# Seven products of a feature transform in another order, with their operands loaded in fewer transfers

## The chip, the cores and the metric

The kernel runs on one core of one Trainium2 chip. The metric is device time in microseconds of one launch. A core has TensorE (PE in the profile, with its weight loads as PEld), VectorE (DVE), ScalarE (ACT), GpSimd (POOL) and SyncE (SP). SP issues nearly all transfers between the chip's memory and the on-chip tiles.

## The reference

Two mixers of the same tokens are blended by a gate. S is 2048 tokens, D 640 features, H 32 heads of 20.

```python
g = sigmoid((x * gate_w).sum(-1, keepdims=True))
qkv = x @ wqkv                                  # 32 heads of 20
o = softmax(q @ k.T * 20 ** -0.5) @ v           # per head
a = o @ wo
A, B = x @ hid_re.T, x @ hid_im.T               # transform of the features
b = seq_re @ A - seq_im @ B                     # transform of the tokens
out = g * a + (1 - g) * b
```

## The kernel before

**Stages.** A prologue (to about 228 us) makes q, k and v, stores them, and makes the right operands of the feature transform. Then comes one long loop of 256 cycles, which carries the attention of all 16 pairs of heads; the transforms are filled into it. A cycle takes the order of its work from the string `ORDER`: `e` is a score matmul with its exponential (L1069, L1075), `m` a score matmul for the maxima of a later unit (L191, L193), `F` a place for one or more groups of transform matmuls, and `B` the burst of sixteen matmuls with v (L714) that closes the cycle. A pair of heads takes 16 cycles of four steps each. The score matmuls of `m` run 43 steps ahead of those of `e` (`LEAD`), so they come to the next pair of heads at the start of the sixth of the sixteen cycles.

**The feature transform** fills the first 56 cycles. It is computed by seven products of half-size blocks in place of eight, as in the known seven-product scheme for matrices. `FEATURE` has a row for each product: the terms of its left operand (sign, half of the tokens, half of the features of x), the terms of its right operand (of the transform's matrices), a factor, and its targets (sign, half of the tokens, real or imaginary part). A product takes eight cycles: the first four with the first half of the columns, the last four with the second. In each cycle `hid_pair` runs 30 matmuls of L498, for one of four blocks of rows. Each product therefore uses two right operands, called sets here (0 to 13).

**Left operands** (tile x from the tiles part). `load_left` is called at a product's first cycle for the next product. It loads the terms of x (in_xh) in three pieces of 1024, 1024 and 512 columns, and works them off in five slabs of 512 columns in the product's first six cycles: with two terms GpSimd adds them (L445), then it splits the sum in a rounded part and a rest (L130, L131).

**Right operands** (tile wb). The prologue made them and stored them in w_scr. `load_right` loads a set, 1600 KB, while the set before it is in use; there are two tiles, so a load can start when the matmuls with the set before that are done, and it has the four cycles of one set to land.

**Targets.** ScalarE and VectorE take the result out of the accumulators. Two of the four targets (half and part both 0, or both 1) are kept on the chip as tiles x and summed by GpSimd (L511). The other two go to memory (a_scr). Where such a target has a value already, this *old value* is loaded into one of three slots (part<-a_scr, 320 KB) at the pair's cycle, added to, and stored again about ten steps later; the load three pairs later, which takes the slot again, waits for that store.

**The k, q and v of the next pair of heads** are loaded at the start of every sixteenth cycle, so at the start of the first, third, fifth and seventh product: six loads each of k and q (kst and qst, 160 KB each), and one of v. They are in the queue from the moment that the scores have done with the tile.

**What sets the order of transfers.** All of them go through one queue, SP's, in the order in which the program wrote them: `at_step` puts an issue at a step of the loop. SP issues each as soon as what it waits for is there, and everything behind it waits as well. Lines 1004 (before) and 1006 (after) are only where `begin` carries out what was put at a step.

Of the kernel before, what the change touches and what calls it, by code (L numbers as in the profile page):

```python
# [13 lines left out]
ALU = mybir.AluOpType  # L14
# [4 lines left out]
P = 128  # L19
# [4 lines left out]
ND = D // P  # L24
# [38 lines left out]
FEATURE = (  # L63
# [7 lines left out]
)  # L71
SETS = 2 * len(FEATURE)
# [11 lines left out]
def f32(ap):  # L84
    return ap.bitcast(F32)
# [3 lines left out]
def mix_kernel(ctx: ExitStack, tc: tile.TileContext, xa, xh, wqk, wb, wr, cdft, wo, out):  # L89
    nc = tc.nc  # L90
    pe, act, dve, pool, sp = nc.tensor, nc.scalar, nc.vector, nc.gpsimd, nc.sync
# [59 lines left out]
    def raw_tile():  # L151
        return work.tile([P, 1024], F32, name="raw", bufs=3)
# [24 lines left out]
    def at_step(i, fn):  # L177
        later.setdefault(i, []).append(fn)
# [243 lines left out]
    def load_right(k):  # L422
        w = wide.tile([P, 2, ND, BW], R, name="wb", bufs=2).rearrange("p z d c -> p (z d c)")[:, : 2 * RW]
        w = w.rearrange("p (z c) -> p z c", z=2)
        rights[k] = w.rearrange("p z (d c) -> p z d c", d=ND)
        return [functools.partial(sp.dma_start, f32(w)[64 * h : 64 * h + 64, z], w_scr[k, z]) for z in range(2) for h in range(2)]

    stages = []

    def load_left(n, stage):  # L430
        terms = FEATURE[n][0]
        hi, lo = [block(z, 2 + n % 2) for z in range(2)]

        def load(q):
            c = slice(1024 * q, min(1024 * q + 1024, ND * 512))
            raws = stage(q)
            for raw, (_, th, dh) in zip(raws, terms):
                sp.dma_start(raw[:, : c.stop - c.start], xh[th, dh, :, c])
            return raws

        def slab(j, raws):
            c = slice(512 * j, 512 * j + 512)
            a, b = [raw[:, j % 2 * 512 : j % 2 * 512 + 512] for raw in raws]
            if len(terms) > 1:
                pool.tensor_tensor(a, a, b, op=ALU.add if terms[1][0] > 0 else ALU.subtract)  # L445
            split(hi[:, c], lo[:, c], a, pool, pool)

        lefts[n] = [l.rearrange("p (d c) -> p d c", d=ND) for l in (hi, lo)]
        raws = {}

        def step_(j):
            def fn():
                if j < 2:
                    raws[j] = load(j)
                if j:
                    slab(j - 1, raws[(j - 1) // 2])
                if j == 2:
                    raws[2] = load(2)
            return fn

        return [step_(j) for j in range(ND + 1)]

    def own_stage(q):
        return [f32(stages[q % 2])[:, z] for z in range(2)]

    def raw_stage(q):
        return [raw_tile()] * 2

    def acc(ri, hf, k):
        if (ri, hf) not in accs:  # L470
# [5 lines left out]
    def hid_pair(u):  # L476
        n, hf, k = u // 8, u // 4 % 2, u % 4
        _, _, factor, targets = FEATURE[n]
        ps = [new_y(z)[:, :HE] for z in range(2)]
        fresh = [(th, ri, hf, k) not in seen for _, th, ri in targets]  # L480
        seen.update((th, ri, hf, k) for _, th, ri in targets)
        rows = [a_scr[ri, hf, th, k] for _, th, ri in targets]
        olds = []
        for (_, th, ri), new, row in zip(targets, fresh, rows):
            old = None
            if th == ri:
                old = acc(ri, hf, k)
            elif not new:
                old = slots.pop(0)
                slots.append(old)  # L490
                at_step(now[0] + 4, functools.partial(sp.dma_start, old, row))
            olds.append(old)
        done_ = 0
        for d in range(ND):
            for a, b in ((0, 0), (0, 1), (1, 0)):
                for z in range(2):
                    r = slice(64 * z, 64 * z + 64)
                    pe.matmul(ps[z], lefts[n][a][r, d, k * P : k * P + P], rights[2 * n + hf][r, b, d],  # L498
                              start=done_ == 0, stop=done_ == 3 * ND - 1)
                done_ += 1  # L500
                if done_ < 3 * ND:
                    yield
        direct = [i for i, ((_, th, ri), new) in enumerate(zip(targets, fresh)) if new and th == ri]
        m = olds[direct[0]] if direct else raw_tile()[:, : 2 * HE].rearrange("p (s c) -> p s c", s=2)

        def read():
            act.activation(m[:, 0], ps[0], AF.Copy, scale=factor)
            dve.tensor_scalar(m[:, 1], ps[1], factor, 1.0, op0=ALU.mult, op1=ALU.mult)  # L508

        def add(sign, old):  # L510
            pool.tensor_tensor(old, old, m, op=ALU.add if sign > 0 else ALU.subtract)  # L511

        extras.append((now[0], read))
        last = n == len(FEATURE) - 1
        for (sign, th, ri), new, row, old in zip(targets, fresh, rows, olds):
            if not new:
                extras.append((now[0] + 3, functools.partial(add, sign, old)))
            if th != ri or ri == 0 and n == len(FEATURE) - 2 or ri == 1 and last:
                at_step(now[0] + (4 if new else 11), functools.partial(sp.dma_start, row, m if new else old))
        yield  # L520

# [64 lines left out]
    for m, (n, t) in enumerate(tiles):  # L586
        qk_pairs(order[n], t, m)
        if m == 8:
            load_v(0)
        if m == 4:  # L590
            sets = load_weights(1)
            queue_sets()
        if n < 5 and t == 1:
            fin()
            if n + 3 < len(order):
                fin = load_wqk(order[n + 3], pool)
        if m == 19:
# [29 lines left out]
    at = {}  # L627
# [610 lines left out]
```

## Time and profile before

| | us |
|---|---|
| runs: median of 3 (lowest to highest) | 1882.21 (1882.14 to 1882.55) |
| the profiled execution, device time | 1880.69 |
| its span, first to last instruction | 1878.8 |
| TensorE busy | 1845.9 (98%) |
| VectorE busy | 1459.4 (78%) |
| GpSimd busy | 1300.1 (69%) |
| ScalarE busy | 1237.4 (66%) |
| TensorE waiting for wb at L498 | 23.4, in 4 waits |

A row of the timeline has the start in us from the span's beginning, the duration in us, the engine, the line, the operation, what it writes and reads (tile<-tiles), and how many instructions were merged in it (x16). In brackets stands how long the engine was idle before, and what ended that. SPq is SP's queue: a row there is the issue of a transfer, and how long the issue took, not the transfer itself. In the list of transfers, KB is 1024 bytes.

A row of a list of waits has who waited for whom, the total in us, the number of waits and the longest.

A row of a table by windows has the window, its length, the busy time of TensorE, its weight loads, VectorE, ScalarE and GpSimd (each with its number of instructions), the TensorE clock that was granted, the busy share of the transfer engines and the GB/s that they moved.

### The profile page before, as it was taken

What the parts mean: (1) busy time and instruction counts of PE and PEld (TensorE: products, weight loads), DVE (VectorE), ACT (ScalarE), POOL (GpSimd) and SP (SyncE); (2) the same over time, 40 slices, a digit from 0 to 9 for tenths busy, and PEclk for the clock granted to TensorE, in tenths of its full rate; (3) what the DMA queues carried; (4) which work ended last, traced back from release to release, by engine and by line L of the source; (5) the groups of instructions that cost most, each with busy time, mean ns of one, the idle gap of its engine ahead of it and who ended that gap; (6) DMA issues with size and microseconds to landing.
All of it is one profiled execution on the core that took longest, in us unless ns stands there. A gap on an engine that the chain in (4) does not pass through costs nothing. (4 is left out here: it accounts for less than half of the span.)

```text
span 1878.8 us, 45939 instructions
## 1 busy us (share of the span) xinstructions
PE 1845.9 (98%) x17917; PEld 1344.8 (72%) x17917; DVE 1459.4 (78%) x2428; ACT 1237.4 (66%) x2378; POOL 1300.1 (69%) x1098
## 2 busy tenths in 40 slices
PE   9999999898899999999999999999999999999998
PEld 8988977675576777767677776677767677776666
DVE  4157589787687888888888888888888888889953
ACT  4233477676576676767677676667767667677785
POOL 1379535573775999466799889968779987734344
PEclk9999999999899999999999999999999999999999
DMA  7887874877776674546557586647486756542224
GB/s 233 202 271 283 270 214 114 193 228 179 201 202 181 207 232 150 159 132 181 183 161 248 156 246 184 196 126 205 138 231 212 209 176 169 167 107 70 63 56 152
DMA packets 195133, 342.26 MB, mean 182 GB/s; under 512 B 54639, under 2 KB 108015, under 8 KB 194659
## 3 DMA queue, kind: packets, MB, share of 16 engines
q1 hardware_dynamic: 193955, 337.35, 61.5%
q0 software_dynamic: 960, 1.97, 0.6%
q8 instruction: 141, 2.31, 0.5%
q14 instruction: 77, 0.63, 0.1%
HBM read 257.79 MB, written 81.28 MB: 180 GB/s over the span
## 5 line engine op out<-in xcount | busy, mean ns | idle before, releaser
L193 DVE TENSOR_REDUCE mx<-ps 128x1 f32<-128x512 f32 x2048 | 1299.7, 686 | 232.4 <-PE ps L191 211.0
L1075 ACT ACTIVATE p<-ps 128x512 f32<-128x512 f32 x2048 | 1088.4, 598 | 454.4 <-PE ps L191 223.5
L191 PE MATMUL ps<-kst,qst 60*128 60x512 f32 x2048 | 778.4, 414 | 2.0 <-DVE mx L193 1.4
L1069 PE MATMUL ps<-qst,kst 62*128 62x512 f32 x2048 | 697.4, 415 | 0.0
L795 PE MATMUL yp<-x,part 64*128 64x320 f32 x5376 | 643.0, 306 | 0.0
L795 PEld LDWEIGHTS yp<-x,part 64*128 64x128 f32 x5376 | 580.7, 186 | 7.4
L1069 PEld LDWEIGHTS ps<-qst,kst 62*128 62x128 f32 x2048 | 334.5, 185 | 222.6 <-DVE mx L193 129.8
L714 PE MATMUL av<-p,v 128*21 128x512 f32 x4096 | 492.5, 596 | 0.0
L191 PEld LDWEIGHTS ps<-kst,qst 60*128 60x128 f32 x2048 | 368.5, 185 | 14.2 <-DVE mx L193 1.6
L131 POOL TENSOR_TENSOR part<-raw,part 128x1024 fp32r<-128x1024 f32 (+3 forms) x134 | 297.1, 2217 | 10.2
L714 PEld LDWEIGHTS av<-p,v 128*21 128x21 f32 x4096 | 95.3, 100 | 207.5 <-issue 206.9
L498 PE MATMUL yp<-wb,x 64*128 64x320 f32 x1680 | 214.7, 314 | 23.4 <-DMA wb<-w_scr 23.4
L130 POOL CAST part<-raw 128x1024 fp32r<-128x1024 f32 (+2 forms) x127 | 125.2, 986 | 131.9 <-PE yp L795 100.7
L656 POOL TENSOR_TENSOR raw<-raw,raw 128x1024 f32<-128x1024 f32 x78 | 187.2, 2400 | 33.4 <-DMA raw<-in_cdft 18.1
L498 PEld LDWEIGHTS yp<-wb,x 64*128 64x128 f32 x1680 | 186.4, 191 | 27.9 <-DMA wb<-w_scr 24.7
L131 POOL TENSOR_TENSOR x<-araw,x 128x320 fp32r<-128x320 f32 x96 | 84.0, 875 | 7.7
L866 PE MATMUL yp<-x,part 64*128 64x320 f32 x720 | 87.3, 309 | 0.0
L883 POOL TENSOR_TENSOR x<-x,m 128x320 f32<-128x320 f32 x30 | 26.2, 874 | 81.0 <-DVE m L878 62.5
L511 POOL TENSOR_TENSOR x<-x,raw 128x640 f32<-128x640 f32 x40 | 62.5, 1563 | 22.8 <-DVE raw L508 16.0
L866 PEld LDWEIGHTS yp<-x,part 64*128 64x128 f32 x720 | 75.7, 185 | 2.6
L689 POOL TENSOR_TENSOR araw<-araw 128x320 f32<-128x320 f32 x80 | 70.1, 876 | 3.2 <-DMA araw<-a_scr 3.2
L511 POOL TENSOR_TENSOR part<-part,raw 128x640 f32<-128x640 f32 x16 | 25.0, 1563 | 53.5 <-DMA part<-a_scr 34.7
(107 smaller groups left out, 1402.5 us busy)
## 6 DMA issues: line engine op xcount, KB each, us to landing
raw<-in_cdft SPq DMA_DIRECT2D x189, 512.0 KB
araw<-a_scr SPq DMA_DIRECT2D x176, 160.0 KB
wb<-w_scr SPq DMA_DIRECT2D x56, 400.0 KB
qk_scr<-p SPq DMA_DIRECT2D x40, 512.0 KB
kst<-qk_scr SPq DMA_DIRECT2D x90, 160.0 KB
qst<-qk_scr SPq DMA_DIRECT2D x90, 160.0 KB
part<-in_xh SPq DMA_DIRECT2D x22, 512.0 KB
yt<-y_scr SPq DMA_DIRECT2D x64, 160.0 KB
```

The costliest lines, as they stand in the source:

```text
L130: e1.tensor_copy(dst1, src)
L131: e2.tensor_tensor(dst2, src, f32(dst1), op=ALU.subtract)
L191: pe.matmul(ps, q[b : b + KROWS, qt * P : (qt + 1) * P], k[b : b + KROWS, kc * 512 : (kc + 1) * 512], start=True, stop=True)
L193: return lambda: dve.tensor_reduce(mx[n][:, h, qt, kc : kc + 1], ps, axis=AX.X, op=ALU.max)
L498: pe.matmul(ps[z], lefts[n][a][r, d, k * P : k * P + P], rights[2 * n + hf][r, b, d], start=done_ == 0, stop=done_ == 3 * ND - 1)
L511: pool.tensor_tensor(old, old, m, op=ALU.add if sign > 0 else ALU.subtract)
L656: pool.tensor_tensor(raws[0], raws[0], raws[1], op=ALU.add if PRODUCTS[n][0][1][0] > 0 else ALU.subtract)
L714: pe.matmul(av[32 * j : 32 * j + DH + 1, :], v[:, kt, h * (DH + 1) : (h + 1) * (DH + 1)], pp[qc][:, h, :], start=kt == 0, stop=kt == NS - 1)
L795: pe.matmul(yp[h][:, :HE], c[r, cz, cs], a[r, az], start=s == 0 and z == 0, stop=s == NS - 1 and z == 2)
L866: pe.matmul(yp[h][:, :HE], o[r, oz, d], wos[d, hf][r, wz], start=d == 0 and z == 0, stop=d == ND - 2 and z == 2)
L1069: pe.matmul(pt, k[b : b + KROWS + 2, kt * P : (kt + 1) * P], q[b : b + KROWS + 2, qc * 512 : (qc + 1) * 512], start=True, stop=True)
L1075: act.activation(pts[n, kt, qc][:, h], pt, AF.Exp, scale=float(DH) ** -0.5)
```

## The change

The products stand in another order: the fifth becomes the third, the third the fourth, the sixth the fifth, and the fourth the sixth. With it, the old values are loaded in the fourth and sixth product; before, in the third and fifth. A right operand is loaded in two transfers of 800 KB, one for each half of the partitions, instead of four of 400 KB, and the second stands four steps behind the first. Both terms of a left operand come in one transfer for each piece. A target that stays on the chip is stored when its last product is done, which a small table now tells.

```diff
 FEATURE = (
     (((1, 1, 1),), ((1, 1, 0), (-1, 0, 0)), 1.0, ((1, 0, 0), (1, 1, 0))),
     (((1, 0, 0), (1, 1, 1)), ((1, 0, 0), (-1, 1, 1)), 1.0, ((1, 0, 0), (1, 1, 1))),
+    (((1, 0, 0), (1, 0, 1)), ((1, 1, 1),), -1.0, ((-1, 0, 0), (1, 0, 1))),
     (((1, 1, 0), (1, 1, 1)), ((1, 0, 0),), 1.0, ((1, 1, 0), (-1, 1, 1))),
+    (((1, 0, 1), (-1, 1, 1)), ((1, 1, 0), (-1, 1, 1)), 1.0, ((1, 0, 0),)),
     (((1, 0, 0),), ((1, 1, 1), (-1, 0, 1)), 1.0, ((1, 0, 1), (1, 1, 1))),
-    (((1, 0, 0), (1, 0, 1)), ((1, 1, 1),), -1.0, ((-1, 0, 0), (1, 0, 1))),
-    (((1, 0, 1), (-1, 1, 1)), ((1, 1, 0), (-1, 1, 1)), 1.0, ((1, 0, 0),)),
...
# load_right
-        return [functools.partial(sp.dma_start, f32(w)[64 * h : 64 * h + 64, z], w_scr[k, z]) for z in range(2) for h in range(2)]
+        return [functools.partial(sp.dma_start, f32(w)[64 * h : 64 * h + 64], w_scr[k].rearrange("z r c -> r z c")) for h in range(2)]
...
# load_left
-            raws = stage(q)
-            for raw, (_, th, dh) in zip(raws, terms):
-                sp.dma_start(raw[:, : c.stop - c.start], xh[th, dh, :, c])
+            raws = stage(q)[:, : len(terms), : c.stop - c.start]
+            at = sorted(2 * th + dh for _, th, dh in terms)
+            sp.dma_start(raws, xh[at[0] : at[-1] + 1 : max(at[-1] - at[0], 1), :, c].rearrange("t p c -> p t c"))
...
# hid_pair
-        last = n == len(FEATURE) - 1
+        ends_ = {(th, ri): i for i, f in enumerate(FEATURE) for _, th, ri in f[3]}
...
-            if th != ri or ri == 0 and n == len(FEATURE) - 2 or ri == 1 and last:
+            if th != ri or ends_[th, ri] == n:
...
# prologue
-        if 20 <= m < 28:
+        if 20 <= m < 28 and m % 2 == 0:
             chunks.pop(0)()
...
# end
-                        at_step(i + 1 + 3 * q, fn)
+                        at_step(i + 1 + 4 * q, fn)
```

What this does to SP's queue is seen at three places. The first is the start of the third product. Ahead of these rows stand four or five loads of k, one piece of x, the first part of wb, and v. Before (wb is the right operand, in_xh is x, qk_scr holds k and q, a_scr the targets):

```order
L1004 DMA wb<-w_scr 64x1600
L438 DMA part<-in_xh 128x1024
L1004 DMA kst_91<-qk_scr 20x4x512
L1004 DMA qst_93<-qk_scr 20x4x512 x2
L1004 DMA wb<-w_scr 64x1600
L1004 DMA part<-a_scr 128x640
L1004 DMA qst_93<-qk_scr 20x4x512
L731 DMA lc<-l_scr 128x16
L438 DMA part<-in_xh 128x512
L1004 DMA qst_93<-qk_scr 20x4x512 x2
L1004 DMA wb<-w_scr 64x1600
L1004 DMA qst_93<-qk_scr 20x4x512
```

The same stretch now:

```order
L438 DMA part<-in_xh 128x2x1024
L1006 DMA kst_91<-qk_scr 20x4x512
L1006 DMA wb<-w_scr 64x2x1600
L1006 DMA a_scr<-raw 128x640
L1006 DMA qst_93<-qk_scr 20x4x512 x3
L733 DMA lc<-l_scr 128x16
L438 DMA part<-in_xh 128x2x512
L1006 DMA qst_93<-qk_scr 20x4x512
L1006 DMA a_scr<-raw 128x640
L1006 DMA qst_93<-qk_scr 20x4x512 x2
```

The last part of wb stood behind five loads of q and two old values; now it stands ahead of all loads of q. The pieces of x have two terms here instead of one, stores of a new target have come in, and the loads of old values are gone.

The second place is the start of the fifth product. Before:

```order
L438 DMA part<-in_xh 128x1024 x2
L1004 DMA a_scr<-raw 128x640
L1004 DMA kst_92<-qk_scr 20x4x512
L1004 DMA wb<-w_scr 64x1600
L1004 DMA kst_92<-qk_scr 20x4x512 x2
L1004 DMA part<-a_scr 128x640
L558 DMA v<-v_scr 128x672
L1004 DMA kst_92<-qk_scr 20x4x512
L728 DMA l_scr<-o 4x512
L1004 DMA wb<-w_scr 64x1600
L438 DMA part<-in_xh 128x1024 x2
```

Now:

```order
L438 DMA part<-in_xh 128x1024
L1006 DMA kst_92<-qk_scr 20x4x512
L1006 DMA wb<-w_scr 64x2x1600
L1006 DMA kst_92<-qk_scr 20x4x512 x2
L1006 DMA a_scr<-part 128x640
L560 DMA v<-v_scr 128x672
L1006 DMA kst_92<-qk_scr 20x4x512
L730 DMA l_scr<-o 4x512
L438 DMA part<-in_xh 128x1024
L1006 DMA kst_92<-qk_scr 20x4x512
L1006 DMA wb<-w_scr 64x2x1600
```

x has one term here now, and in the place of the loads of old values stand stores of those that the fourth product added to.

The third place is the start of the seventh product, where pieces of a for the token transform (part<-a_scr 128x4x320, 640 KB) are loaded as well. Before:

```order
L1004 DMA wb<-w_scr 64x1600
L697 DMA part<-a_scr 128x4x320
L1004 DMA kst_91<-qk_scr 20x4x512
L1004 DMA qst_93<-qk_scr 20x4x512 x2
L1004 DMA wb<-w_scr 64x1600
L1004 DMA a_scr<-x_3090 128x640
L1004 DMA qst_93<-qk_scr 20x4x512
L731 DMA lc<-l_scr 128x16
L1004 DMA qst_93<-qk_scr 20x4x512 x2
L1004 DMA wb<-w_scr 64x1600
L1004 DMA qst_93<-qk_scr 20x4x512
```

Now, from a little further ahead:

```order
L1006 DMA part<-a_scr 128x640
L1006 DMA a_scr<-part 128x640
L1006 DMA kst_91<-qk_scr 20x4x512 x2
L1006 DMA wb<-w_scr 64x2x1600
L1006 DMA kst_91<-qk_scr 20x4x512 x2
L1006 DMA a_scr<-part 128x640
L560 DMA v<-v_scr 128x672
L1006 DMA kst_91<-qk_scr 20x4x512
L730 DMA l_scr<-o 4x512
L699 DMA part<-a_scr 128x4x320
L1006 DMA kst_91<-qk_scr 20x4x512
L1006 DMA wb<-w_scr 64x2x1600
```

The last load of an old value of the sixth product has come in ahead of the loads of k, and the second half of wb stands ahead of all loads of q, where the last quarter stood behind five of them.

More of the change, by code (lines that the diff above doesn't have):

```diff
@@ L442, in slab @@
             c = slice(512 * j, 512 * j + 512)
-            a, b = [raw[:, j % 2 * 512 : j % 2 * 512 + 512] for raw in raws]
+            parts = [raws[:, z, j % 2 * 512 : j % 2 * 512 + 512] for z in range(len(terms))]
+            a = parts[0]
             if len(terms) > 1:
-                pool.tensor_tensor(a, a, b, op=ALU.add if terms[1][0] > 0 else ALU.subtract)
+                one, two = parts if terms[0][1:] < terms[1][1:] else parts[::-1]
+                pool.tensor_tensor(a, one, two, op=ALU.add if terms[1][0] > 0 else ALU.subtract)
             split(hi[:, c], lo[:, c], a, pool, pool)
@@ L463, in own_stage @@
     def own_stage(q):
-        return [f32(stages[q % 2])[:, z] for z in range(2)]
+        return f32(stages[q % 2])
     def raw_stage(q):
-        return [raw_tile()] * 2
+        return raw_tile().rearrange("p (z c) -> p z c", z=1)
     def acc(ri, hf, k):
@@ L1214 @@
     wqk = w[:, : 2 * D].reshape(ND, P, 2 * ND, P).transpose(2, 1, 0, 3)
-    xh = np.asarray(A_x)[0].reshape(2, 2, 512, 2, ND, 64).transpose(0, 3, 1, 5, 4, 2).reshape(2, 2, P, ND * 512)
+    xh = np.asarray(A_x)[0].reshape(2, 2, 512, 2, ND, 64).transpose(0, 3, 1, 5, 4, 2).reshape(4, P, ND * 512)
     wr = np.stack([np.asarray(m) for m in (B_dft_hid_re, B_dft_hid_im)])
```

## The prediction

> **What bounds the kernel now.** I read the span first, then whom TensorE waits for, then its timeline around each of those waits.
>
> ```profile
> span 1878.8 us, 45939 instructions
> PE yp L498 <- DMA wb<-w_scr: 23.4, 4, 8.8
> ```
>
> TensorE is the bound, and over the span it waits for one thing worth speaking of: a right operand of the feature products (wb, read by the matmuls of L498), four times, 23.4 us. A cycle ends with sixteen matmuls of L714, so the distance between two such rows is the length of a cycle.
>
> ```profile
> 346.69 1.92 PE L714 MATMUL av<-p,v 128*21 128x512 f32 x16
> 352.94 1.92 PE L714 MATMUL av<-p,v 128*21 128x512 f32 x16
> 361.52 1.43 PE L498 MATMUL yp<-wb,x 64*128 64x320 f32 x7 [5.72 <-DMA wb<-w_scr]
> 366.69 1.92 PE L714 MATMUL av<-p,v 128*21 128x512 f32 x16
> ...
> 460.69 1.92 PE L714 MATMUL av<-p,v 128*21 128x512 f32 x16
> 468.23 0.63 PE L498 MATMUL yp<-wb,x 64*128 64x320 f32 x1 [4.83 <-DMA wb<-w_scr]
> 477.67 1.43 PE L498 MATMUL yp<-wb,x 64*128 64x320 f32 x7 [8.80 <-DMA wb<-w_scr]
> 482.80 0.63 PE L714 MATMUL av<-p,v 128*21 128x512 f32 x4
> ...
> 576.91 1.92 PE L714 MATMUL av<-p,v 128*21 128x512 f32 x16
> 583.80 1.43 PE L498 MATMUL yp<-wb,x 64*128 64x320 f32 x7 [4.01 <-DMA wb<-w_scr]
> 590.24 1.05 PE L714 MATMUL av<-p,v 128*21 128x512 f32 x8
> ...
> 353.00:366.70 13.70, 7.98 (x65) 5.85 (x64) 5.65 (x11) 4.76 (x9) 8.65 (x8) 0.75 0.65 153
> ```
>
> A plain cycle is 6.25 us (346.69 to 352.94). Three cycles, in the third, fifth and seventh product, take 13.75, 22.11 and 13.33 us: 7.50, 15.86 and 7.08 too long, **30.4 us together**. The waits in them are 5.72, 13.63 and 4.01; the other 1.78, 2.23 and 3.07 (mean 2.4) is slow work after each wait: the last row (PEclk is the third number from its end) has a granted clock of 0.75 in the long cycle.
>
> Why the operand is late stands in the timeline of the queue that issues it.
>
> ```profile
> 326.50 0.29 SPq L1004 DMA_DIRECT2D kst<-qk_scr  x1
> ...
> 350.36 0.45 SPq L1004 DMA_DIRECT2D wb<-w_scr  x1
> 352.53 0.28 SPq L1004 DMA_DIRECT2D qst<-qk_scr  x1
> 353.67 0.34 SPq L1004 DMA_DIRECT2D part<-a_scr  x1
> 354.48 3.01 SPq L752 DMA_DIRECT2D o_scr<-o  x4
> 358.52 0.35 SPq L1004 DMA_DIRECT2D a_scr<-part  x1
> 364.12 0.34 SPq L1004 DMA_DIRECT2D part<-a_scr  x1
> SPq L752 <- DMA part<-in_xh: 4.5, 5, 1.5
> ```
>
> The last quarter of wb is issued at 350.36 and lets TensorE go at 361.52, 11.2 us later. Seven issues follow it and then none until it has landed; and a store of o_scr waits for x to land, which it has no use for (last row). So SP keeps eight transfers under way and issues the next when the one eight places before lands. The queue is full, and what counts is how many bytes stand ahead.
>
> ```profile
> kst<-qk_scr SPq DMA_DIRECT2D x90, 160.0 KB
> wb<-w_scr SPq DMA_DIRECT2D x56, 400.0 KB
> part<-in_xh SPq DMA_DIRECT2D x22, 512.0 KB
> part<-a_scr SPq DMA_DIRECT2D x16, 320.0 KB
> v<-v_scr SPq DMA_DIRECT2D x16, 336.0 KB
> part<-a_scr SPq DMA_DIRECT2D x4, 640.0 KB
> ```
>
> From the first k load (326.50) to 361.52 these landed: 11 k and q loads 1760 KB, x 1280, wb 1600, two old values 640, v 336, two of 8: 5632 KB in 35.0 us, **161 KB/us**. The fifth product has two terms of x and a store more: 7232 KB from 434.35 to 477.67, **167 KB/us**. The seventh, from 548.11 to 583.80, has four stores, three pieces of a of 640 KB, 11 k and q loads, wb and v: 6912 KB, **194 KB/us**.
>
> ```profile
> 434.35 0.29 SPq L1004 DMA_DIRECT2D kst<-qk_scr  x1
> ...
> 548.11 0.37 SPq L1004 DMA_DIRECT2D a_scr<-x  x1
> ```
>
> **The change, part by part.** *Fewer, larger transfers.* 28 wb issues and 15 of x go; the bytes stay. SP's own issuing (0.3 to 0.5 us a row) is hidden, since in the bad stretches SP waits for landings. What it brings is position: both halves of wb now stand ahead of all q loads, and count for two places of the eight instead of four.
>
> *Old values out of the third and fifth product.* They met the k, q and v loads there; the fourth and sixth have none. I price each stretch by its bytes.
>
> Third product, to the second half of wb: 6 k loads 960, x in two parts of 1024, wb 1600, v 336, l 8: 4952 KB. It must land by 355.80 (361.52 less 5.72), 29.3 us after 326.50, which takes 169 KB/us. At 161 it is 1.5 us late, at 167 it is 0.4 late, at the 183 found below 2.2 early. I take: in time.
>
> But the third product now prepares a left operand of two terms, 1280 KB more of x, and **the q loads are late next**. The scores of L191, which run ahead, read the new k and q from the start of the sixth cycle of an odd product. The first product shows it:
>
> ```profile
> 230.89 0.40 SPq L1004 DMA_DIRECT2D kst<-qk_scr  x1
> ...
> 249.39 1.95 SPq L1004 DMA_DIRECT2D qst<-qk_scr  x2
> ...
> 260.64 0.50 PE L191 MATMUL ps<-kst,qst 60*128 60x512 f32 x1
> ...
> 390.00:415.00 25.00, 25.00 (x250) 17.22 (x248) 21.79 (x37) 18.20 (x37) 22.51 (x19) 1.00 0.93 293
> ```
>
> There 12 k and q loads, x 2560, v and two stores, 5456 KB, were in by 260.64, since TensorE did not wait: at most 29.75 us, at least **183 KB/us**. The third product gets exactly this and wb on top: 7072 KB with l and lc. Its sixth cycle would start at 352.94 + 6.25 + 1.85 = 361.04, so it has 34.5 us, and needs 205 KB/us. Low end: wb's 1600 KB at the 286 KB/us (293 GB/s, last row) of a stretch without k and q add 5.6 us to 29.75: 0.8 us late. High end: all at 161: 9.4 late. I take 183, since the mix is the first product's: 38.6 us, **4.1 late**, and with 2.4 of slow work **6.5 us**. Before, the last q load was issued behind the last wb (352.53 against 350.36, above), so it landed after 361.52 and was late too, covered by the wait for wb.
>
> [...]
>
> Fifth product: one term of x (1280), no old values after its k loads but two stores: 5792 KB in the same 34.5 us. At 161: 1.5 late; at 167: 0.2; at 183: 2.9 early. I take 0.
>
> Seventh: no change but one old value left from the sixth (320 KB), and the last q load counted: 7392 KB from 548.11. At its own 194: 586.2, and needed at 576.91 + 6.25 + 1.85 = 585.0: **1.2 late**, at 183 3.5 late, at 205 early. A wait this short I take without slow work after it.
>
> [...]
>
> *Fourth and sixth product* now carry eight old loads and eight stores each beside wb and x, without k and q; the stretch of 293 GB/s has stores, wb and x, so I price them at nothing. If that cover is gone, the nearest price is the shortest of the three losses, 7.08 a product. *Left operand on GpSimd:* the same instructions in all, two terms in products 2, 3, 4, 5 and 7. *The loads in the prologue* come two places earlier; TensorE has no wait for them.
>
> Sum against the profiled execution's 1880.69: less 30.4, plus 6.5, 0 and 1.2: **1858.0**. The median of the runs, 1882.21, lies 1.5 above that execution, which is inside the range.
>
> **Rivals.** *Everything hidden.* The first product landed before 260.64, how much is not seen; with 4 us of slack there nothing waits. For it: the fewer places held by wb. Against: wb beside k and q went at 161 and 167. 1880.69 - 30.4 = 1850.3.
>
> *The old rate stays.* wb and k, q share the engines as before, at 161 KB/us: third 9.4 + 2.4, fifth 1.5, seventh 3.5 + 2.4 = 19.2 left, 1869.5. For it: two stretches measured it. Against: both held old values, whose loads wait for stores.
>
> *Slower, by GpSimd.* Its queue is in order, and an addition waits for the old value:
>
> ```profile
> 452.15 1.57 POOL L511 TENSOR_TENSOR part<-part,raw 128x640 f32<-128x640 f32 x1 [5.91 <-DMA part<-a_scr]
> 453.68 1.28 POOL L445 TENSOR_TENSOR part<-part 128x512 f32<-128x512 f32 x1
> 455.02 0.62 POOL L130 CAST x<-part 128x512 fp32r<-128x512 f32 x1
> 455.72 1.29 POOL L131 TENSOR_TENSOR x<-part,x 128x512 fp32r<-128x512 f32 x1
> ...
> 469.12 1.53 POOL L511 TENSOR_TENSOR part<-part,raw 128x640 f32<-128x640 f32 x1 [10.59 <-DMA part<-a_scr]
> ```
>
> The fourth and sixth product have 16 additions (1.57) and five slabs (3.19): 41.1 of 50 us. Waits of 5.91 and 10.59 through all eight pairs, 33 us in pairs of two, would end them 24 late; the slabs are queued in the first six of eight cycles, so two (12.5) absorb half, and the next left operand stops TensorE for 11.5 + 2.4 in each: 27.8, with the 19.2 above 47.0, against 30.4 gained: 1897.3. It decides from about 18 us late on. Against: both waits fell under k and q loads.
>
> *It does nothing:* the wait moves whole to the next late load, 1880; nothing in the bytes says so.
>
> **How the numbers follow.** Forecast, 1853 to 1863: 0.48. All hidden: 0.25. Old rate: 0.20. GpSimd: 0.04. Nothing: 0.03. The range reaches from all hidden to just under the old rate, **1850 to 1868**. A difference of 0.2% (3.8 us) is what the measurement can tell; faster 0.94, same 0.02, slower 0.04.
>
> **What would show it.** Right: no waits of L498 for wb; one wait of L191, or of the matmuls beside it, for qst in the sixth cycle of the third product, some 4 us, and a cycle of about 12.7 us there; the fifth product plain. All hidden: every cycle 6.25. Old rate: that cycle near 18 us, and wb late too. GpSimd: TensorE waits for x at L498. Wrong is the argument by bytes if the fourth or sixth product waits, where no k and q are loaded.

## The result, and the profile after

| | before | after |
|---|---|---|
| median of 10 runs each, us | 1882.18 (1874.82 to 1885.65) | 1872.46 (1868.36 to 1879.49) |
| profiled execution, its device time, us | 1880.69 | 1871.42 |
| its span, us | 1878.8 | 1869.6 |

The ratio of after to before is 0.9955, with an interval of 0.9941 to 0.997: about 9.7 us less, where 22.7 were forecast (from the 1880.69 of the profiled execution to 1858.0). The time lies above the predicted range of 1850 to 1868.

The head of the list of TensorE's waits after the change:

```profile
core 0 of [0], span 1869.6 us
engine line waited for: us in total, times, longest us
PE ps L191 <- DVE mx L193: 10.8, 4, 5.9
PE yp L500 <- ACT raw L509: 3.3, 2, 2.7
PE yp L500 <- DMA wb<-w_scr: 1.6, 1, 1.6
```

In this execution the wait for wb has gone from 23.4 us to 1.6, as the change meant; in a second one of the same kernel, further down, it is 7.9. And two waits that were 1.4 us and nothing have become 14.1: the score matmuls of L191 now wait for VectorE's maxima, and the products (L500, before L498) wait for ScalarE, which empties their accumulator. Neither of these is a transfer by name. The timeline of the third, the fifth and the seventh product and of one place in the token transform, with TensorE's, VectorE's and SP's rows put together in order of time, shows what they wait for:

```profile
346.70 0.35 SPq L733 DMA_DIRECT2D lc<-l_scr  x1
355.23 1.91 PE L716 MATMUL av<-p,v 128*21 128x512 f32 x16
357.65 0.49 DVE L510 TENSOR_SCALAR raw<-yp 128x320 f32<-128x320 f32 x1 [1.10 <-DMA a_scr<-raw]
361.85 0.25 DVE L736 RECIPROCAL lc<-lc 128x16 f32<-128x16 f32 x1 [2.24 <-DMA lc<-l_scr]
362.70 0.50 PE L191 MATMUL ps<-kst,qst 60*128 60x512 f32 x1 [1.81 <-DVE mx L193]
364.47 3.50 PE L716 MATMUL av<-p,v 128*21 128x512 f32 x16
372.30 1.06 PE L716 MATMUL av<-p,v 128*21 128x512 f32 x8
...
456.57 0.34 SPq L733 DMA_DIRECT2D lc<-l_scr  x1
460.01 1.92 PE L716 MATMUL av<-p,v 128*21 128x512 f32 x16
464.12 0.38 PE L500 MATMUL yp<-wb,x 64*128 64x320 f32 x1 [1.62 <-DMA wb<-w_scr]
468.25 0.25 DVE L736 RECIPROCAL lc<-lc 128x16 f32<-128x16 f32 x1 [2.75 <-DMA lc<-l_scr]
469.10 0.49 PE L191 MATMUL ps<-kst,qst 60*128 60x512 f32 x1 [2.32 <-DVE mx L193]
471.23 3.02 PE L716 MATMUL av<-p,v 128*21 128x512 f32 x16
...
581.89 2.40 POOL L677 TENSOR_TENSOR wb<-wb 128x1024 f32<-128x1024 f32 x1 [10.87 <-PE av L716]
590.73 0.44 ACT L509 ACTIVATE raw<-yp 128x320 f32<-128x320 f32 x1 [3.46 <-POOL x L513]
591.22 0.47 PE L500 MATMUL yp<-wb,x 64*128 64x320 f32 x2 [2.74 <-ACT raw L509]
595.40 1.92 PE L716 MATMUL av<-p,v 128*21 128x512 f32 x16
...
1185.89 0.25 DVE L736 RECIPROCAL lc<-lc 128x16 f32<-128x16 f32 x1 [6.11 <-DMA lc<-l_scr]
1186.74 0.79 PE L191 MATMUL ps<-kst,qst 60*128 60x512 f32 x1 [5.87 <-DVE mx L193]
```

Read the first block from the bottom. L191 waits for a maximum. On VectorE the reciprocal of lc (L736) stands ahead of those maxima in the program, and it waits 2.24 us for a transfer of 8 KB; the score matmul starts 0.85 us after the reciprocal does. That transfer was issued at 346.70, fifteen microseconds before, and lc is there at 361.85. It is small, but it stands in the same full queue as wb did. In the same cycle VectorE waits for the store of a raw tile (a_scr<-raw), again the same queue. The second block shows it in the fifth product, with a piece of the old wait for wb left. The third block is another chain: GpSimd gets to its work on the token transform's matrix late (L677), and an addition into a target (L513) stands behind it; ScalarE waits for that, and TensorE for ScalarE. The bracket of L677 names TensorE, but the landing of the matrix's two loads, read from their semaphores, is 581.73, right ahead of 581.89 (581.08 ahead of 581.24 in the kernel with all partitions, below). The fourth block, in the token transform, is the first chain again: VectorE waits 6.11 us for lc.

A wait has a tail here too. The cycle from 364.47 to 372.30 has no wait, and yet took 7.83 us where 6.25 is plain, at a granted clock of 0.79 (PEclk, third from the end). The second row shows that half the clock was granted for 3.42 us, just after a wait of 1.81 us:

```profile
364.47:372.30 7.83, 7.83 (x63) 4.58 (x63) 5.71 (x11) 4.54 (x9) 3.42 (x3) 0.79 0.92 253
364.29:367.71 3.42, 3.42 (x18) 0.52 (x16) 2.12 (x5) 1.42 (x3) 3.16 (x4) 0.50 0.78 270
```

Cycles are numbered from 0 below, each from one burst of L714 (L716 after) to the next. This is how much longer than 6.25 us the long ones were in the two profiled executions:

| place | before | after | forecast for after |
|---|---|---|---|
| first burst later than before's 233.80 | 0 | 2.3 | 0 |
| third product, cycles 19 and 20 | 7.5 | 3.0 + 1.6 | 6.5 |
| fifth product, cycles 35 and 36 | 15.9 | 5.0 + 1.1 | 0 |
| seventh product, cycle 51 | 7.1 | 1.1 | 1.2 |
| seventh product, cycle 54 | 0 | 3.0 | 0 |
| token transform, cycle 147 | 1.7 | 7.6 | as before |

The first five rows are 17.1 us, where before had 30.4; cycle 147 has 5.9 more than before; the rest of the program took 1.7 less. 30.4 - 17.1 - 5.9 + 1.7 = 9.1, the difference of the spans (9.2).

### The profile page after: what moved, and what is told of

The parts are those of the page before. It is cut to its first block, busy times and chain, and to the rows that moved or that the text cites. A ratio compares the mean times of both kernels' runs of the same rounds, so it can differ in the third digit from the quotient of the medians.

```text
span 1869.6 us, 45887 instructions
## 1 busy us (share of the span) xinstructions
PE 1844.7 (99%) x17917; PEld 1339.1 (72%) x17917; DVE 1459.2 (78%) x2428; ACT 1236.0 (66%) x2378; POOL 1300.1 (70%) x1098
## 5 line engine op out<-in xcount | busy, mean ns | idle before, releaser
L191 PE MATMUL ps<-kst,qst 60*128 60x512 f32 x2048 | 778.7, 414 | 11.1 <-DVE mx L193 10.8
L1071 PE MATMUL ps<-qst,kst 62*128 62x512 f32 x2048 | 695.8, 414 | 0.0
L716 PE MATMUL av<-p,v 128*21 128x512 f32 x4096 | 495.3, 599 | 0.0
L1071 PEld LDWEIGHTS ps<-qst,kst 62*128 62x128 f32 x2048 | 333.3, 185 | 223.0 <-DVE mx L193 131.5
L191 PEld LDWEIGHTS ps<-kst,qst 60*128 60x128 f32 x2048 | 368.2, 184 | 23.6 <-DVE mx L193 11.9
L716 PEld LDWEIGHTS av<-p,v 128*21 128x21 f32 x4096 | 95.6, 100 | 209.5 <-issue 208.5
L500 PE MATMUL yp<-wb,x 64*128 64x320 f32 x1680 | 209.3, 308 | 4.9 <-ACT raw L509 3.3
L500 PEld LDWEIGHTS yp<-wb,x 64*128 64x128 f32 x1680 | 180.8, 186 | 8.9 <-ACT raw L509 3.9
L513 POOL TENSOR_TENSOR x<-x,raw 128x640 f32<-128x640 f32 x40 | 62.5, 1562 | 29.9 <-DVE raw L510 17.8
L447 POOL TENSOR_TENSOR part<-part 128x512 f32<-128x512 f32 x25 | 32.3, 1292 | 46.1 <-PE ps L191 22.8
```

Of the source, the lines that this page charges most:

```text
L191: pe.matmul(ps, q[b : b + KROWS, qt * P : (qt + 1) * P], k[b : b + KROWS, kc * 512 : (kc + 1) * 512], start=True, stop=True)
L716: pe.matmul(av[32 * j : 32 * j + DH + 1, :], v[:, kt, h * (DH + 1) : (h + 1) * (DH + 1)], pp[qc][:, h, :], start=kt == 0, stop=kt == NS - 1)
L1071: pe.matmul(pt, k[b : b + KROWS + 2, kt * P : (kt + 1) * P], q[b : b + KROWS + 2, qc * 512 : (qc + 1) * 512], start=True, stop=True)
```

## The experiments

Each was timed in several rounds beside the kernel before, on the same chip. The runs were spread over three chips: order and merging alone, lc late and the second run of the change on one; one term of x, the prologue's quarters, quarters by turns and all partitions on another; the rest on a third. So two kernels are best compared by their ratios to the kernel before. "Fifth product's loads" is the time from the issue of its first k load to the landing of its last q load, read from the semaphores; "third product's loads" likewise. Their bytes are those counted in the prediction: 5792 and 7072 KB.

**One part of the change at a time.** First the order of the products alone, with the loads as before:

```diff
+    (((1, 0, 0), (1, 0, 1)), ((1, 1, 1),), -1.0, ((-1, 0, 0), (1, 0, 1))),
     (((1, 1, 0), (1, 1, 1)), ((1, 0, 0),), 1.0, ((1, 1, 0), (-1, 1, 1))),
+    (((1, 0, 1), (-1, 1, 1)), ((1, 1, 0), (-1, 1, 1)), 1.0, ((1, 0, 0),)),
     (((1, 0, 0),), ((1, 1, 1), (-1, 0, 1)), 1.0, ((1, 0, 1), (1, 1, 1))),
-    (((1, 0, 0), (1, 0, 1)), ((1, 1, 1),), -1.0, ((-1, 0, 0), (1, 0, 1))),
-    (((1, 0, 1), (-1, 1, 1)), ((1, 1, 0), (-1, 1, 1)), 1.0, ((1, 0, 0),)),
...
-            if th != ri or ri == 0 and n == len(FEATURE) - 2 or ri == 1 and last:
+            if th != ri or ends_[th, ri] == n:
```

> The new order of the products alone, with the transfers as they were before. Theory A (the queue's pace is set by bytes, and the order takes the old values out of the k, q and v loads): most of the gain is here; the three long cycles of before (13.75, 22.11, 13.33 us) shrink in the third and fifth product, and the seventh stays at 11 to 13; time 1872 to 1876. Rival B (it is the merging, which lets wb stand ahead of q): the third and fifth product still wait for wb, 5 to 15 us each, and the time is within 3 us of before (1879 to 1885).

Measured: 1885.14 us, ratio 1.0016 (1.0001 to 1.003). TensorE waits for wb as before, over its whole span:

```profile
PE yp L498 <- DMA wb<-w_scr: 25.4, 5, 7.9
```

Then the merged transfers alone (x too, as in the change's diff), in the order of before:

```diff
-        return [functools.partial(sp.dma_start, f32(w)[64 * h : 64 * h + 64, z], w_scr[k, z]) for z in range(2) for h in range(2)]
+        return [functools.partial(sp.dma_start, f32(w)[64 * h : 64 * h + 64], w_scr[k].rearrange("z r c -> r z c")) for h in range(2)]
...
-                        at_step(i + 1 + 3 * q, fn)
+                        at_step(i + 1 + 4 * q, fn)
```

> The merged transfers alone, with the old order of the products. Theory A: the third and fifth product still have old values and k, q, v loads together; wb comes earlier, so the waits for wb fall to 0 to 4 us, but lc, q or x are late in their place: cycles of 9 to 14 us there; time 1874 to 1879. Rival B: it gets all of the change's gain, 1870 to 1874. Both: the end of the prologue is some 2 us later than before, if the larger loads ahead of the stores of q and k are the cause, and not otherwise.

Measured: 1882.85 us, ratio 1.0004 (0.9989 to 1.002); the first burst came at 236.19.

```profile
PE ps L1071 <- DMA qst<-m_scr: 11.7, 3, 6.1
PE ps L191 <- DVE mx L193: 5.3, 4, 2.2
PE yp L500 <- DMA wb<-w_scr: 3.6, 1, 3.6
```

Neither part gains anything alone. The order alone did nearly what rival B said, with wb late as before; the merging alone did worse than both theories. With the merging alone wb is nearly in time, and the wait goes to loads of 4 KB (qst<-m_scr, the maxima that the scores of L1071 read). Both together bring 0.45%. So the two parts do not add up; the wait moves to whatever in the queue is needed next. That old values stand ahead of these small loads in the third and fifth product, and the new order takes them away, fits this; it was not tried apart.

**Taking away the new wait.** If the reciprocal of lc is the price, it can be done later (its step is the third number):

```diff
-        steps = (6, 10, 18, 25, 29, 36, 46) if n < NU - 2 else (1, 4, 10, 12, 15, 19, 21)
+        steps = (6, 10, 24, 25, 29, 36, 46) if n < NU - 2 else (1, 4, 10, 12, 15, 19, 21)
```

> The changed kernel with the reciprocal of each unit's sums (VectorE, which waits there for lc) put at step 24 instead of 18 after the unit's end. Theory C (VectorE, waiting for lc in order, holds up the maxima and so the scores of L191): the wait of 5.9 us near 1187 and the waits of 1.8, 2.3 and 0.8 us in the third, fifth and seventh product go; the q loads bind next in the third and fifth product, so 1 to 3 us of the latter come back; time 6 to 9 us below the changed kernel, 1863 to 1867. Rival D (the wait for lc only shows what the late queue would cost anyway): within 2 us of the changed kernel.

Measured: 1873.6 us, ratio 0.9952 (0.9935 to 0.997), the same as the change itself. The wait for lc is gone, and others are there in its place, first in the third product, then in the fifth:

```profile
367.36 0.47 PE L191 MATMUL ps<-kst,qst 60*128 60x512 f32 x1 [1.54 <-DMA a_scr<-raw]
...
469.31 0.60 PE L500 MATMUL yp<-wb,x 64*128 64x320 f32 x1 [6.04 <-DMA wb<-w_scr]
```

Cycles 19, 20 and 35 took 7.58, 9.76 and 14.62 us. So rival D holds: the pace of the whole queue is the price, and lc only the first to be hit.

**The changed kernel once more**, to see what differs from one execution to the next.

> The changed kernel once more, for a second trace. Theory E (the waits near 1187 us, at the start and in the prologue differ from run to run, since no instruction there was changed): the long cycle in the token transform's third product takes 6.3 to 10 us instead of 13.84, the prologue's end varies by 2 us. Rival F (they are the change's own): the long cycle is again 13 to 14.5 us and the prologue's end again 2 us later than before.

Measured: 1874.19 us, ratio 0.9964 (0.9952 to 0.9977). The head of TensorE's waits:

```profile
PE yp L500 <- DMA wb<-w_scr: 7.9, 2, 5.8
PE ps L191 <- DVE mx L193: 5.6, 4, 2.2
```

wb is late again: 5.8 us in the fifth product, where cycle 35 alone was 9.0 us too long (15.26), and 2.0 in the seventh, where cycles 51 and 52 took 12.78 and 7.73 us, 8.0 too long together. The third product was 3.5 us too long, and cycle 54 was plain. Cycle 147 took 9.21 us instead of 13.84, and in the other kernels of this study between 6.3 and 10.6 (6.3 in one of two executions with quarters by turns, 7.89 in the other); before had 7.93. So most of what cycle 147 shows is chance. The first burst came at 235.90 again, 2.1 us after before's: that part is the change's own.

**Fewer bytes in one stretch.** The second term of x for the fourth product is left out (GpSimd uses the first in its place): 1280 KB less in the third product's stretch, in as many transfers.

```diff
             at = sorted(2 * th + dh for _, th, dh in terms)
+            if n == 3:
+                raws, at = raws[:, :1], at[:1]
...
-            parts = [raws[:, z, j % 2 * 512 : j % 2 * 512 + 512] for z in range(len(terms))]
+            parts = [raws[:, 0 if n == 3 else z, j % 2 * 512 : j % 2 * 512 + 512] for z in range(len(terms))]
```

> The changed kernel without the second term of x for the fourth product: 1280 KB of the 7072 KB in the third product's stretch are not loaded, at the same number of transfers, and GpSimd adds the first term to itself in its place, so the output differs. Theory H (bytes decide in the third product): its last q load lands 6 to 7 us earlier, 30 to 32 us after the first k load; the cycles of 9.24 and 7.83 become plain (6.3), about 4 us of gain, 1868 to 1870. Rival (the number of places and the landing of each decide): the q loads land within 2 us of the 37.8 us of the changed kernel and its long cycles stay. The fifth and the seventh product, which load the same as in the changed kernel, stay as they were.

Measured: 1865.02 us, ratio 0.9904 (0.9887 to 0.992). Cycle 19 took 6.99 us and 20 was plain, so fewer bytes do help the third product, but its loads took 34.47 us, between the two expectations. The gain of the whole is more than these cycles explain (3.8 us); where the rest comes from is not shown (cycle 147 took 7.18 us here, the fifth product was 9.9 too long, and the changed kernel was not timed on this chip). The number to keep is another: **1280 KB less shortened the stretch by only 3.3 us** (37.8 to 34.5), some 388 KB/us, while the 5792 KB that stay went at 168. In this stretch, kilobytes did not cost the same. x is loaded into all 128 partitions, wb into 64 at a time, k and q into 20.

That led to the theory called G in what follows, a guess at this point: a transfer into half of the partitions holds the queue up for longer than its bytes say.

**The loads of the prologue.** The first two right operands in quarters again, in the prologue alone:

```diff
-        if 20 <= m < 28 and m % 2 == 0:
+        if 20 <= m < 28:
...
+        if quarters:
+            return [functools.partial(sp.dma_start, f32(w)[64 * h : 64 * h + 64, z], w_scr[k, z]) for z in range(2) for h in range(2)]
```

> The changed kernel with the loads of the first two right operands in the prologue in four quarters each again, one place apart, as before; in the loop nothing differs. Theory P (the loop starts later because the 800 KB loads hold up the stores of q and k): first burst at 233.8 to 234.1 instead of 235.9 to 236.8, no wait of ScalarE for a store above 3 us before it, and the time 2 us lower than the changed kernel, near 1870 to 1871. Theory Q (the two merged kernels merely had a slow start, or the larger x load does it): first burst 235.9 to 236.8 and no gain. The cycles behind are as in the changed kernel, within the some 5 us by which its executions differ.

Measured: 1868.96 us, ratio 0.9928 (0.9903 to 0.9954), but the first burst at 235.30, later than Theory P allows. The fifth product waited 5.5 us for wb. This run alone doesn't settle the prologue; the table further down does better.

**Quarters everywhere**, two at each of the change's two places, lower and upper half of the partitions by turns; and the control, with the same quarters in the other sequence, lower twice and then upper twice:

```diff
-        return [functools.partial(sp.dma_start, f32(w)[64 * h : 64 * h + 64], w_scr[k].rearrange("z r c -> r z c")) for h in range(2)]
+        return [functools.partial(sp.dma_start, f32(w)[64 * h : 64 * h + 64, z], w_scr[k, z]) for z in range(2) for h in range(2)]
...
-                        at_step(i + 1 + 4 * q, fn)
+                        at_step(i + 1 + 4 * (q // 2), fn)
```

```diff
-        return [functools.partial(sp.dma_start, f32(w)[64 * h : 64 * h + 64, z], w_scr[k, z]) for z in range(2) for h in range(2)]
+        return [functools.partial(sp.dma_start, f32(w)[64 * h : 64 * h + 64, z], w_scr[k, z]) for h in range(2) for z in range(2)]
```

By turns, first run:

> The changed kernel with every right operand in four quarters, two at each of the two places, in the sequence of before: lower half of the partitions, upper half, lower, upper. Same places, same bytes. [...]

By turns, again:

> The kernel with alternating quarters once more, beside the other sequence on the same chip. If its 1861.9 is real: 1859 to 1865, first burst 233.7 to 234.5. If it was a lucky place: 1866 to 1872 and the first burst at 235 to 236.

One half twice:

> The kernel with alternating quarters, with the quarters in the other sequence: lower half of the partitions twice, then the upper half twice, as an 800 KB transfer has them. Theory G2 (the alternation is what brought 11 us): fifth product's loads 37 to 39 us, time 1869 to 1874 as in the changed kernel. Rival G3 (the alternation is nothing, smaller transfers or the prologue brought it): within 3 us of 1861.9, fifth product 35 to 36 us.

Measured: by turns 1861.85 us, ratio 0.9886 (0.9866 to 0.9906), and 1859.05, ratio 0.9867 (0.9845 to 0.9889); one half twice 1865.05, ratio 0.9908 (0.9882 to 0.9934). Quarters by turns beat the change's halves at the same places by 0.7 to 1.0%, and quarters with one half twice by some 0.5%, though they take four of the queue's eight places instead of two: the count of places did not decide it. How much of it the sequence brings and how much the size is not settled, since the intervals of the two sequences overlap.

Nor is it shown that the gain comes from the pace of the stretches. The signs that theory G names for the pair after this one are the fifth product's loads within 33 us and packets of wb of 350 to 450 ns. Here the loads took 35.3 and 32.6 us by turns, 38.2 with one half twice, and 35.6 to 38.0 in six executions with 800 KB halves; packets of wb took 548 and 521 ns by turns. The third product's loads took 37.3 and 37.2 us by turns, 36.5 with one half twice and 37.5 to 38.1 with halves. So those signs were absent in the first run by turns, and the test of theory G is the next pair.

In the prologue the sequence shows more clearly. First burst of each profiled execution:

| loads of the first two right operands | first burst, us |
|---|---|
| quarters by turns (before, order alone, the prologue's quarters, quarters by turns twice) | 233.80, 233.99, 235.30, 233.73, 233.91 |
| quarters, one half twice | 236.56 |
| halves of 800 KB (the change twice, lc late, merging alone, one term of x) | 236.11, 235.90, 236.77, 236.19, 235.77 |

The means of the first and the last row are 234.1 and 236.1.

**All 128 partitions.** Each right operand is stored twice by the prologue, and loaded in two transfers of 800 KB that each fill all partitions. The count, the size and the places of the loads are the change's. The control has the same doubled stores, and loads by halves as the change does.

```diff
-    w_scr = dram.tile([SETS, 2, 64, RW], F32, name="w_scr")
+    w_scr = dram.tile([SETS, 2, P, RW], F32, name="w_scr")
...
-                stores.append((w_scr[k, z].rearrange("r (q c) -> (r q) c", q=2), part))
+                for h in range(2):
+                    stores.append((w_scr[k, z, 64 * h : 64 * h + 64].rearrange("r (q c) -> (r q) c", q=2), part))
...
-        return [functools.partial(sp.dma_start, f32(w)[64 * h : 64 * h + 64], w_scr[k].rearrange("z r c -> r z c")) for h in range(2)]
+        return [functools.partial(sp.dma_start, f32(w)[:, z], w_scr[k, z]) for z in range(2)]
```

> The changed kernel with each right operand stored twice in the prologue, once for each half of the partitions, so that it is loaded in two transfers of 800 KB that each cover all 128 partitions. Same count, size and places of the loads in the loop; the prologue has 11.2 MB more to store. Theory G: packets of wb take 350 to 450 ns instead of 590 to 680, the fifth product's loads are in within 33 us, its long cycles 11.22 and 7.35 (3 to 9 us too long in the executions so far) are plain to within 1 us, and from the first burst to the last row the kernel takes 4 to 8 us less. Rival (the halves do not matter): packets as long as before, the fifth product as late. The prologue: up to 30 us longer if the stores cannot hide, which is read apart from the loop by the first burst.

> Control for the kernel whose right operands were stored twice: the same doubled stores in the prologue, but loaded by halves of the partitions as in the changed kernel. Theory G (what helped was that each transfer covers 128 partitions): the fifth product's loads take 35 to 38 us again and wb's packets near 600 ns, its cycles are 4 to 9 us too long together; first burst near 246, time 1877 to 1884, 12 us above the 1865.8 of the other. Rival (it was the later start, or the copies in memory): the loads are in within 30 us and the time is within 3 us of 1865.8.

Measured: 1865.79 us, ratio 0.9907 (0.9888 to 0.9927), and for the control 1884.58 us, ratio 1.0 (0.9983 to 1.0018). Between the two kernels lies what a load fills (all partitions with one part of the operand, or half of them with both parts), and **18.8 us**; the chips differ too, and by the ratios it is 0.9%. The next kernel settles the chip. First TensorE's waits from 240 to 620 us with all partitions, then the head of the control's:

```profile
PE yp L501 <- ACT raw L510: 3.0, 1, 3.0
PE ps L191 <- DMA qk_scr<-p: 0.3, 1, 0.3
```

```profile
PE yp L501 <- DMA wb<-w_scr: 6.5, 2, 4.5
PE yp L501 <- ACT raw L510: 3.8, 2, 2.0
PE ps L191 <- DVE mx L193: 1.6, 1, 1.6
```

And a row by windows for the fifth product's loads, all partitions and control (the last two numbers are the busy share of the transfer engines and GB/s):

```profile
442.37:470.29 27.92, 27.92 (x283) 19.96 (x276) 24.13 (x41) 20.56 (x42) 19.92 (x18) 1.00 0.86 250
```

```profile
448.26:483.89 35.63, 32.06 (x318) 22.34 (x314) 27.80 (x47) 23.69 (x48) 21.23 (x18) 1.00 0.90 201
```

The control's engines were busier and moved less. The loads of the same 5792 KB took 27.9 us against 35.6, those of the third product 32.0 against 38.1, and with all partitions TensorE was busy for the whole window (27.92 of 27.92). Cycles 19 to 53 are plain; only cycle 54 (9.49 us) and cycle 147 (10.62) are long, and cycle 54 is the chain over GpSimd, which has no k or q in it. The doubled stores cost the prologue 10 us: the first burst came at 246.17, and at 248.67 in the control.

**Only where it pays.** The five right operands that load beside k and q (sets 5, 6, 9, 10 and 13) are doubled and fill all partitions; the others load in quarters by turns.

```diff
+WHOLE = (5, 6, 9, 10, 13)
...
-                for h in range(2):
+                for h in range(2 if k in WHOLE else 1):
...
+        if k in WHOLE:
+            return [functools.partial(sp.dma_start, f32(w)[:, z], w_scr[k, z]) for z in range(2)]
...
```

> The changed kernel with only the five right operands doubled that are loaded beside k and q in the third, fifth and seventh product (sets 5, 6, 9, 10 and 13); these load in two transfers over 128 partitions, the others in quarters as in the kernel with alternating quarters. 4 MB more to store instead of 11.2. Theory G: cycles 16 to 53 plain to 1 us, fifth product's loads in within 29 us; first burst at 236 to 240; time 1855 to 1861. Rival (the prologue pays back what the loop gains): first burst above 243, time 1864 or more.

Measured: **1858.71 us**, ratio 0.9853 (0.983 to 0.9875), 1.5% faster than the kernel before and, ratio against ratio, 1.0% faster than the change. The first burst came at 235.65, and cycles 16 to 53 are plain. The timeline and the list of TensorE's waits from 240 to 620 us:

```profile
354.77 1.91 PE L721 MATMUL av<-p,v 128*21 128x512 f32 x16
361.01 1.49 PE L721 MATMUL av<-p,v 128*21 128x512 f32 x12
...
455.11 1.92 PE L721 MATMUL av<-p,v 128*21 128x512 f32 x16
461.54 1.91 PE L721 MATMUL av<-p,v 128*21 128x512 f32 x16
```

```profile
PE yp L505 <- ACT raw L514: 0.9, 1, 0.9
```

The fifth product's loads took 30.2 us, not within the 29 expected, and that is early enough; the third's took 30.6. This run was on the control's chip, where halves took 35.6 and 38.1, so the chip is not what shortens the stretches. Its gain over the kernel with quarters by turns is not settled: 0.9853 (0.983 to 0.9875) and 0.9867 (0.9845 to 0.9889) were measured side by side.

## Why the prediction was wrong, point by point

**The mechanism held in part.** SP did keep eight transfers under way: a q load was issued at 464.00, when the half of wb eight places before it had landed at 463.99. Faster by over 0.2% came true, and in the third product wb is no longer waited for. But "no waits of L498 for wb" failed: 1.6 us in the profiled execution and 7.9 in the next. The step that failed is the price of the stretches, and most of all the sentence on the fifth product: "At 161: 1.5 late; at 167: 0.2; at 183: 2.9 early. I take 0."

- **Fifth product: 0 forecast, 6.1 us measured** (9.0 in the next execution). Its 5792 KB took 35.7 us, 162 KB/us, the low end. The 183 came from the first product, whose stretch holds 2560 KB of x and no wb; the fifth has half of that x, and wb. By the run without a term of x, x costs a third to a half of what the rest costs per byte (388 KB/us against 168), so by these rates a stretch with less x goes slower than the mean of a stretch with more. One rate for all bytes was the error, and what the runs showed in its place is that the form of the wb loads counted: the same 5792 KB took 27.9 us when each load of wb filled all 128 partitions, and 35.6 in the control, where each filled 64. The landing of wb itself was worked out only for the third product; in the fifth the second half landed at 463.99, and TensorE waited 1.62 us for it. And lateness cost more than itself: 1.62 and 2.32 us of waits made 6.1, with a granted clock of 0.50 for 3.41 us behind them. The prediction took a short wait without slow work after it; 1.81 us in the third product had such a tail too, and 0.82 in the seventh had none (granted clock 1.00 from 566.2 to 573.6).
- **Third product: 6.5 forecast, 4.6 measured.** The rate was right there (7072 KB in 37.8 us, 187 KB/us; forecast 38.6), since its mix has two terms of x. But the late one that counted was not q. lc and a raw tile's store stopped TensorE before the q loads were needed, and while it stood the q loads came in (the last landed at 366.61, and the first scores that read them began at 367.90). That the loss came out near the forecast is in part luck. The prediction counted lc's 8 KB among the bytes and never asked when lc was needed, nor what stands behind it on VectorE.
- **Seventh product: 1.2 forecast, 1.1 in cycle 51**, though again by lc (the first wait of L191 there is 0.82 us). This agreement is luck: the next execution lost 8.0 us there, with wb 2.0 late, so the seventh product was priced too low as well. Cycle 54, 3.0 us, was not forecast: GpSimd's late work on the token transform.
- **Prologue: 0 forecast, 2.3 measured.** "TensorE has no wait for them" was true of the loads, and not of what stands behind them in the queue, as far as these waits show. ScalarE's waits from 150 to 240 us for the stores of q and k, before:

```profile
ACT p L128 <- DMA qk_scr<-p: 16.5, 8, 2.8
ACT p L369 <- DMA qk_scr<-p: 2.6, 1, 2.6
```

  and after, fewer and longer:

```profile
ACT p L128 <- DMA qk_scr<-p: 12.1, 4, 4.5
ACT p L369 <- DMA qk_scr<-p: 8.9, 3, 3.9
```

- **Fourth and sixth product: 0, right.** No cycle between 23 and 34 or between 38 and 50 is long.
- **The sum.** The profiled execution, 1871.42, missed 1858.0 by 13.4 us: 6.1 of them in the fifth product, 2.3 in the prologue, 3.0 in cycle 54, 5.9 in cycle 147, and some 4 the other way in the rest. Without cycle 147, which is mostly chance, this one execution would have been within the range; the median of ten, 1872.46, was not, and the second profiled execution lost as much in other places.
- **The rivals.** The old rate (1869.5) came nearest, for another reason than it gave: its rate held in the fifth product alone. TensorE never waited for a left operand. Everything hidden (1850.3) is what the loads over all partitions come close to: the best kernel's profiled execution took 1855.7.

The prediction priced wb by its bytes and its place in the queue; its form, half of the partitions to a load, has no term of its own in the sum, before or after. The runs measured what it was worth: with wb over all 128 partitions, 7.7 us less than in the control in the fifth product (35.6 to 27.9) and 6.1 in the third (38.1 to 32.0).

## What to carry to other kernels

When a full queue makes something late, list everything that stands in it, with the time at which each is needed and what stands in order behind the one that waits: here, once the 1600 KB of wb were in time in the third product, the 8 KB of lc took their place. Do not price a mixed stretch at one rate: here the same 5792 KB took 35.6 us with loads of wb into 64 partitions and 27.9 with loads into 128, and the form was worth more than the place (0.9%, against 0.45% for order and merging together). Merging transfers saves places in a queue, but the places were not what counted here: four quarters by turns beat two halves (ratios 0.9886 and 0.9867 against 0.9955). And one execution is no test of a sum of small losses: a term can agree in one and be 7 us off in the next.

## What the runs showed of the hardware

- The same 800 KB, in the same number of transfers at the same places, filled 128 partitions far sooner than 64: packets of 6400 bytes took 360 ns on the mean in the fifth product's stretch against 610 in the control and 623 in the changed kernel, whose operands go in by halves. The first 800 KB of wb landed 9.7 us after their issue there, against 12.3 and 13.2.
- Four quarters that take the halves of the partitions by turns in the prologue went with a loop that began about 2 us earlier than the same bytes with one half at a time (first burst 234.1 on the mean of five against 236.1 of five, and 236.56 for quarters with one half twice).
- Half the granted clock came for 3.41 us behind waits of 1.81 and 2.32 us of TensorE (the change), and of 1.54 us (lc late, where single score matmuls took 0.62 us in place of 0.40 for as long); the wait of 2.74 us in the seventh product had none behind it (granted clock 1.00 from 591.2 to 595). So in these executions the length of a wait alone did not decide it.
- A wait in the token transform (cycle 147) cost 7.6 and 3.0 us in two executions of the changed kernel, and 1.6 us and nothing in two with quarters by turns; one execution of this kernel cannot tell differences of 5 us.
